# Weight loading and splitting of a mixture-of-experts kernel put at fixed places, and part of the routing lists moved into the attention stage

## The chip, the cores and the metric

The kernel runs on one core of a Trainium2 chip. The metric is the device time of one execution in microseconds (us). Engines are named as the profile names them: PE (matrix products), PEld (loading the weights into PE), DVE (vector), ACT (scalar), POOL (the engine that issues the indexed gathers and scatters) and SP (the engine that issues the plain transfers). Each engine works through its own instructions in the order in which they were written.

## The reference, cut to what matters

```python
# attention with a decaying state: 4 batches, 8 heads, 768 steps, head size 48
for t in range(S):
    cur = einsum('bhd,bhe->bhde', u * kt, vt)
    y[:, :, t] = einsum('bhd,bhde->bhe', rt, state + cur)
    state = w * state + einsum('bhd,bhe->bhde', kt, vt)
# mixture of experts on x = y as 3072 tokens of 384; 8 experts, hidden size 1024
noisy = x @ w_gate + log1p(exp(x @ w_noise)) * noise
top2 = the two largest of 8 per token; weights = softmax over the two
for e in range(8):
    h = maximum(x[mask] @ w1[e], 0)
    out[mask] += weight * (h @ w2[e])
```

All inputs and the output are float32. The kernel keeps that accuracy by writing each operand of a large product as a sum of two parts, high and low, and taking three products (high by high, high by low, low by high).

## The kernel before, in words

**Attention** (loop over 24 tiles of 128 tokens, `for i in range(NT)`). Per tile, PE makes transposes, scores (L353) and the output `py` (L395, L403); DVE masks the scores (`am`, L361) and adds up the tile's output `x` (L411), which goes to DRAM as `xd`. PE then makes router logits (L433). The routing of the tokens is done in three groups of 8 tiles by the generator `route(g)`, on DVE mainly: `rstep(us)` runs as many of its small steps as fit into a given time budget, so that they lie between the attention's own DVE operations.

**Lists.** Every expert needs the list of its tokens. `drop` makes a group's contribution: two compare operations for `oa` (L513), three for `ob` (L517, L520, L522), eight small PE products into `pL` (L526), and an addition to `L` (L532). For groups 1 and 2, `route` makes only the contribution to expert 0's list; the contribution to the lists of experts 1 to 7 is made by `rest(g)`, twice per group (first and second choice). Before the change `rest(1)` and `rest(2)` are both queued after the attention stage has ended and run inside the products of expert 0, by `rest_step`. When both are done, `rows` turns `L` into row numbers `GR` (L679), and `xgather(1, 0)` starts to gather expert 1's tokens.

**Experts.** Each expert's 832 places are taken in chunks: expert 0 in three (256, 256 and 320 columns), experts 1 to 7 in two (384 and 448 columns). A chunk has a first product `p1` (8 blocks f of the hidden size, 9 matmuls each into `ph`, L881, three PSUM buffers) and a second product `p2` (24 matmuls for each tile of 128 tokens into `pym`, L915, and 16 for the tile of 64, L906 and L908). After each block of `p1`, ACT takes the relu's high part (`hb`, and `ht` for the last 64 columns, L883) and DVE the low part (L885). After each tile of `p2`, ACT copies `pym` out to `ot` (L921), and `emit_out` scales it by the gate on DVE (L934 for expert 0; L932 for the others, which also adds what was in `out`) and scatters it with POOL (L936). For experts from 2 on, `spread` (L832) rearranges the next chunk's gathered tokens `xgt` into `xq` by 16 transfers on SP, DVE transposes them (L850), and ACT and DVE split them into `xh` and `xl` (L860, L861). `pgather` (L819) fetches the present `out` rows, and `xgather` (L810) the next tokens; both are on POOL.

**Weights.** The weights of an expert come in seven parts: three of `w1` (128x1024 each) and four of `w2` (two blocks of 384 columns each). Each part is loaded by SP into one of three staging buffers `stg` (L278, L281), split by ACT into the high part (L285) and by DVE into the low part (L287). Before the change `w_split` makes a generator per part, and `wstep`, called once after each block of `p1` and each tile of `p2`, moves up to three of them on by one step: load, two empty steps, high part, low part. So a part's high split stands on ACT a few blocks after its load was put on SP's queue, and the first three parts of expert e+1 are begun in expert e's first chunk, the other four in its second.

## Time and profile before

| | us |
|---|---|
| runs before | 660.16, 667.80, 665.02 (median 665.02) |
| profiled execution, its own time | 663.06 |
| its span, first to last instruction | 661.3 |
| PE busy | 620.0 (94% of the span) |
| DVE, ACT, POOL busy | 373.6, 265.1, 263.8 |
| mean granted PE clock | 0.978 of full speed |

The attention stage takes the first 175 us of the span, expert 0 the time up to 247.8 us, and experts 1 to 7 follow with 55 to 60 us each up to 650.4 us. Rows of the timeline give a start in us from the span's beginning, a duration in us, the engine, the line, the operation and what it writes and reads; in square brackets stands how long the engine was idle before it and what ended that idle time. Rows of stretches give the length, the busy time and instruction count of PE, PEld, DVE, ACT and POOL, the granted PE clock as a share of full speed, and the busy share and rate of the DMA engines.

### The profile page before, as it was taken

How to read it: one execution, taken by the hardware profiler on the slowest of the kernel's cores; microseconds unless marked ns; L12 is line 12 of the kernel's file. 1: busy time of each engine (PE TensorE's matmuls, PEld its weight loads, DVE VectorE, ACT ScalarE, POOL GpSimd, SP SyncE). 2: the span in 40 equal slices, each digit the busy share in tenths (PEclk: the TensorE clock that was granted, in tenths of full speed). 3: DMA queues.
4: the chain of work that ended last, by engine and by line, in shares of the span. 5: the costliest groups of instructions: out<-in, count | busy, mean ns of one | idle time of the engine just before them, and what ended most of it. 6: DMA issues, size and time to landing. Idle time of an engine off the chain costs nothing.

```text
span 661.3 us, 12051 instructions
## 1 busy us (share of the span) xinstructions
PE 620.0 (94%) x4310; PEld 588.1 (89%) x4311; DVE 373.6 (56%) x925; ACT 265.1 (40%) x737; POOL 263.8 (40%) x389
## 2 busy tenths in 40 slices
PE   7899899989998789999899999999999999999993
PEld 5789899988898789999799988998999899899993
DVE  8787878699379945253526454462645536254330
ACT  1465656675322524242334334243342424333310
POOL 8587445544201237323532452263254227315111
PEclk8999879999999999999899999999999999999997
DMA  7997657654305534445643745374364446533100
GB/s 125 216 229 169 151 132 166 166 134 129 92 1 151 164 103 119 115 146 130 160 141 111 180 112 166 106 182 149 106 181 120 155 125 162 170 90 105 37 10 29
DMA packets 135350, 86.56 MB, mean 131 GB/s; under 512 B 110625, under 2 KB 125345, under 8 KB 135282
## 3 DMA queue, kind: packets, MB, share of 16 engines
q1 hardware_dynamic: 125346, 56.87, 34.5%
q0 software_dynamic: 9936, 28.83, 14.5%
q8 instruction: 36, 0.59, 0.4%
q14 instruction: 32, 0.26, 0.1%
HBM read 59.03 MB, written 19.76 MB: 119 GB/s over the span
## 4 chain that ended last, share of the span: by engine, by line
PE 35%; SPq 14%; DMA 8%; DVE 7%; ACT 4%; issue 4%; POOL 2%; POOLq 0%; DVEq 0%; ACTq 0%
PE pym L915 17%; PE ph L881 15%; SPq L832 12%; DMA stg<-in_moe_w_dram 5%; SPq L281 2%; DMA pv<-out_dram,GA 2%; DVE xl L861 1%; DMA xgt<-xd,GR 1%; ACT xh L860 1%; POOL pv L819 1%; ACT w1h L285 1%; PE pym L908 1%; DVE ot L932 1%; PE pym L906 1%; DVE hb L885 1%
## 5 line engine op out<-in xcount | busy, mean ns | idle before, releaser
L915 PE MATMUL pym<-w1h,hb 128*128 128x384 f32 x768 | 202.3, 341 | 5.3 <-DVE hb L885 3.5
L885 DVE SCALAR_TENSOR_TENSOR hb<-ph,hb 128x384 fp32r<-128x384 f32 (+1 forms) x136 | 72.4, 533 | 143.4 <-ACT ht L883 83.3
L915 PEld LDWEIGHTS pym<-w1h,hb 128*128 128x128 f32 x768 | 139.8, 190 | 8.5 <-DVE hb L885 5.9
L881 PE MATMUL ph<-xh,w0h 128*128 128x384 f32 (+3 forms) x408 | 141.3, 346 | 5.8 <-DVE ht L885 4.0
L881 PE MATMUL ph<-xl,w0h 128*128 128x384 f32 (+3 forms) x408 | 140.0, 343 | 0.5 <-DVE xl L861 0.4
L881 PE MATMUL ph<-xh,w0l 128*128 128x384 f32 (+3 forms) x408 | 139.6, 342 | 0.0
L936 POOL DMA_INDIRECT out_dram<-ot,TK x56 | 57.5, 1027 | 192.6 <-DVE ot L932 154.7
L915 PE MATMUL pym<-w1l,hb 128*128 128x384 f32 x384 | 130.0, 339 | 0.0
L883 ACT ACTIVATE hb<-ph 128x384 fp32r<-128x384 f32 (+1 forms) x136 | 63.2, 469 | 96.3 <-PE ph L881 95.3
L881 PEld LDWEIGHTS ph<-xh,w0h 128*128 128x128 f32 x408 | 77.3, 189 | 11.0 <-issue 3.3
L881 PEld LDWEIGHTS ph<-xl,w0h 128*128 128x128 f32 x408 | 77.3, 190 | 3.6 <-DVE xl L861 1.2
L881 PEld LDWEIGHTS ph<-xh,w0l 128*128 128x128 f32 x408 | 77.5, 190 | 2.7
L915 PEld LDWEIGHTS pym<-w1l,hb 128*128 128x128 f32 x384 | 72.7, 189 | 0.1
L403 PE MATMUL py<-vt,am 128*128 128x96 f32 x384 | 60.3, 283 | 5.8 <-DVE am L361 4.8
L819 POOL DMA_INDIRECT pv<-out_dram,GA x49 | 53.2, 1085 | 31.0 <-issue 15.4
L810 POOL DMA_INDIRECT xgt<-xd,GR x42 | 43.6, 1038 | 40.9 <-DMA xq<-xgt 25.5
L921 ACT ACTIVATE ot<-pym 128x384 f32<-128x384 f32 x45 | 22.0, 489 | 92.7 <-PE pym L915 92.7
L403 PEld LDWEIGHTS py<-vt,am 128*128 128x128 f32 x384 | 51.7, 197 | 7.8 <-DVE am L361 7.8
L314 POOL TENSOR_TENSOR kd<-kt,tabk 128x192 f32<-128x192 f32 x46 | 27.8, 625 | 61.7 <-PE pwarm L371 50.4
L861 DVE TENSOR_TENSOR xl<-xq,xh 128x384 fp32r<-128x384 f32 (+1 forms) x42 | 22.3, 530 | 31.3 <-ACT xh L860 31.3
L860 ACT ACTIVATE xh<-xq 128x384 fp32r<-128x384 f32 (+1 forms) x42 | 21.0, 500 | 44.9 <-DVE xq L850 44.9
L810 POOL DMA_INDIRECT xg<-xd,GR x14 | 13.7, 982 | 59.6 <-DVE f L688 34.0
(217 smaller groups left out, 910.7 us busy)
## 6 DMA issues: line engine op xcount, KB each, us to landing
stg<-in_moe_w_dram SPq DMA_DIRECT2D x32, 384.0 KB, 4.4
stg<-in_moe_w_dram SPq DMA_DIRECT2D x72, 128.0 KB, 3.4
xq<-xgt SPq DMA_DIRECT2D x144, 36.0 KB, 1.9
rd<-in_r_dram SPq DMA_DIRECT2D x24, 192.0 KB, 4.0
vt<-in_v_dram SPq DMA_DIRECT2D x24, 192.0 KB, 4.0
xd<-x SPq DMA_DIRECT2D x24, 192.0 KB, 2.0
out_dram<-zrow SPq DMA_DIRECT2D x16, 288.0 KB, 3.8
kt<-in_k_dram SPq DMA_DIRECT2D x23, 192.0 KB, 3.6
```

Of the source, the lines that this page charges most:

```text
L314: (eng or nc.gpsimd).tensor_mul(kd[i % 3][:, h, :D], kt[i][:, h], tabk[:, h, :D])
L403: nc.tensor.matmul(o2, AM[i][:, s, p, :], vt[i][:, h, None, :].to_broadcast([128, 2, D]), start=not c and h == 0, stop=h == H - 1, skip_gr ...
L810: nc.gpsimd.indirect_dma_start(out=xg[:n], out_offset=None, in_=xd[:GROUPS[GEARLY - 1][1] * 128] if early_ else xd, in_offset=bass.Indirec ...
L819: nc.gpsimd.indirect_dma_start(out=pv[:n], out_offset=None, in_=out, in_offset=bass.IndirectOffsetOnAxis(ap=GA[:n, e * NJ + t:e * NJ + t + ...
L832: nc.sync.dma_start(xq[32 * a:32 * a + 32, q:w_:4], XGT[e, ci][32 * q:32 * q + 32, :m, a * 96:(a + 1) * 96])
L860: nc.scalar.activation(xh[:, g], v, AF.Copy)
L861: nc.vector.tensor_sub(xl[:, g], v, xh[:, g].bitcast(F32))
L881: nc.tensor.matmul(ph[:, :w_], a[:, d, fs], x[:, :w_ // 32, d], start=(j == 0), stop=(j == len(q) - 1))
L883: nc.scalar.activation(h_[:, f, 0, :], ph[:, a:b], AF.Relu)
L885: nc.vector.scalar_tensor_tensor(h_[:, f, 1, :], ph[:, a:b], 0.0, h_[:, f, 0, :].bitcast(F32), op0=ALU.max, op1=ALU.subtract)
L915: nc.tensor.matmul(py, hb[:, f, a, hs], x[:, f, :], start=(j == 0), stop=(j == len(q) - 1))
L936: st = nc.gpsimd.indirect_dma_start(out=out, out_offset=bass.IndirectOffsetOnAxis(ap=TK[:n, q:q + 1], axis=0), in_=ot[:n], in_offset=None, ...
```

## The change

It does five things:

1. **Weight parts at fixed places.** `wstep` is kept for expert 0 alone. For the others `w_p2`, called ahead of each second product, puts three loads on SP's queue (parts 0 to 2 of expert e+1 ahead of every second product but the last of expert e; parts 4 to 6 ahead of the last), and `w_p1`, called after each block j of a first product, does the splits: in an expert's first chunk parts 4 to 6 of the same expert at j = 0 to 5 (high part at even j, low part at odd j), in its last chunk parts 0 to 3 of the next expert at j = 0 to 7, with part 3 loaded at j = 2. No split stands in a second product any more.
2. **`rest(1)` begins in the attention stage.** It is queued at tile 22, and what is left of it is finished before `route(2)` is queued. `rest(2)` stays where it was.
3. **Expert 0's scaling** moves from DVE (L934) to ACT.
4. **`spread` is a generator.** Its 16 transfers are put out three at a time, one lot per block of the first product.
5. **Expert 1's first chunk** may be transposed inside expert 0's last second product if the lists are done by then (`next(xt)` twice per tile), and `tile_counts` (a small PE product and nine small DVE operations) moves from the end of expert 0's second chunk to the end of its third.

```diff
-                if mat or e < ESP:
-                    nc.sync.dma_start(tv, src)
-                else:
-                    for a in range(4):
-                        nc.sync.dma_start(tv[32 * a:32 * a + 32, 0, :], src[a])
+                nc.sync.dma_start(tv, src)
...
+    def w_load(e, k):
+        if e >= E:
+            return
+        t = stg.tile([128, 1024], F32, name="stg")
+        WS[e, k] = t
+        if k < ND:
+            if e >= ESP:
+                src = w1[e].rearrange("(a c j) f -> c a j f", a=4, j=32)[k]
+                for a in range(4):
+                    nc.sync.dma_start(t[32 * a:32 * a + 32, :], src[a])
+            else:
+                nc.sync.dma_start(t, w1[e, k * 128:(k + 1) * 128, :])
+        else:
+            c = 2 * (k - ND)
+            nc.sync.dma_start(t[:, :2 * DM].rearrange("p (c d) -> p c d", d=DM),
+                              w2[e, c * 128:(c + 2) * 128, :].rearrange("(c p) d -> p c d", p=128))
...
+    def w_hi(e, k):
+        if e < E:
+            tv, hi, _ = w_view(e, k)
+            nc.scalar.activation(hi, tv, AF.Copy)
+
+    def w_lo(e, k):
+        if e < E:
+            tv, hi, lo = w_view(e, k)
+            nc.vector.tensor_sub(lo, tv, hi.bitcast(F32))
+
+    def w_p1(e, ci, j):
+        if ci == 0:
+            if j < 6:
+                (w_lo if j % 2 else w_hi)(e, ND + 1 + j // 2)
+        elif ci == len(chunks(e)) - 1:
+            k = j // 2
+            (w_lo if j % 2 else w_hi)(e + 1, k)
+            if j == 2:
+                w_load(e + 1, ND)
+
+    def w_p2(e, ci):
+        last = ci == len(chunks(e)) - 1
+        for k in range(ND):
+            w_load(e + 1, ND + 1 + k if last else k)
...
                                   XGT[e, ci][32 * q:32 * q + 32, :m, a * 96:(a + 1) * 96])
+                if (4 * q + a) % 3 == 2:
+                    yield
...
-            nc.vector.tensor_scalar(ot[:n], ot[:n], g, None, op0=ALU.mult)
+            nc.scalar.activation(ot[:n], ot[:n], AF.Copy, scale=g)
...
             if b == i + 1:
+                while g == GEARLY and route_q:
+                    rstep(1)
...
             early()
+            route_q.append(rest(GEARLY - 1))
...
-    tile_counts(CAP)
     att_stack.close()
...
-    wq.extend(w_split(1))
-    for _ in range(3):
-        wstep()
+    w_p2(0, 0)
     att_pool[0] = late[0]
-    route_q.append(rest(GEARLY - 1))
     route_q.append(rest(GEARLY))
...
+        sd = spread(*seq[s + 1]) if sp[0] else iter(())
         for j, _ in enumerate(p1(e, ci)):
             while hold:
                 emit_out(*hold.pop(0))
-            if j == 0 and sp[0]:
-                spread(*seq[s + 1])
+            next(sd, None)
...
-            wstep()
+            w_p1(e, ci, j)
+        for _ in sd:
+            pass
         if s > 2 and s + 2 < len(seq):
             xgather(*seq[s + 2])
+        w_p2(e, ci)
...
+            if s == 2 and listed[0]:
+                for _ in range(2):
+                    next(xt, None)
...
-            wstep()
             hold.append((e, t))
...
             xgather(*seq[s + 2])
+            tile_counts(CAP)
```

How the order of the instructions changes is shown at three places. In these rows stand the line, the operation, what it writes and reads, its shape, and how often it stands in a row; lines are those of each kernel's own file, so that the same operation has another number after the change.

ACT, in the second first product of an expert (448 columns; the same in experts 2 to 6). `hb` and `ht` are the relu of one block, `GT` the gates, `w0h` and `w1h` the high parts of `w1` and `w2`. Before:

```order
L883 ACTIVATE hb<-ph 128x384
L883 ACTIVATE ht<-ph 128x64
L837 ACTIVATE GT<-xgt 128x1 x3
L883 ACTIVATE hb<-ph 128x384
L883 ACTIVATE ht<-ph 128x64
L285 ACTIVATE w1h_4977<-stg 128x768
L883 ACTIVATE hb<-ph 128x384
L883 ACTIVATE ht<-ph 128x64
L285 ACTIVATE w1h_4977<-stg 128x768
L883 ACTIVATE hb<-ph 128x384
L883 ACTIVATE ht<-ph 128x64
L285 ACTIVATE w1h_4977<-stg 128x768
```

And after the change, from the first block on:

```order
L936 ACTIVATE hb<-ph 128x384
L936 ACTIVATE ht<-ph 128x64
L336 ACTIVATE w0h_4958<-stg 128x1024
L936 ACTIVATE hb<-ph 128x384
L936 ACTIVATE ht<-ph 128x64
L936 ACTIVATE hb<-ph 128x384
L936 ACTIVATE ht<-ph 128x64
L890 ACTIVATE GT<-xgt 128x1 x3
L336 ACTIVATE w0h_4958<-stg 128x1024
L936 ACTIVATE hb<-ph 128x384
L936 ACTIVATE ht<-ph 128x64
L336 ACTIVATE w0h_4958<-stg 128x1024
```

The three splits of `w2` in a row, after blocks 3 to 5, are gone; splits of the next expert's `w1`, loaded a whole second product earlier in the program, stand after every second block.

SP, at the same place of the program: `xq<-xgt` are the 16 transfers of `spread`, `32x1024` a quarter of a `w1` part, `128x2x384` a `w2` part. Before:

```order
L281 DMA stg<-in_moe_w_dram 32x1024 x12
L832 DMA xq<-xgt 32x3x96 x16
L278 DMA stg<-in_moe_w_dram 128x2x384 x4
L832 DMA xq<-xgt 32x4x96 x8
L832 DMA xq<-xgt 32x3x96 x8
```

And after the change:

```order
L315 DMA stg<-in_moe_w_dram 32x1024 x12
L883 DMA xq<-xgt 32x3x96 x9
L320 DMA stg<-in_moe_w_dram 128x2x384
L883 DMA xq<-xgt 32x3x96 x7
L320 DMA stg<-in_moe_w_dram 128x2x384 x3
L883 DMA xq<-xgt 32x4x96 x8
L883 DMA xq<-xgt 32x3x96 x8
```

SP's order is nearly what it was; one load of `w2` has moved in among the 16 transfers.

DVE, from the last two attention tiles into expert 0's first product (`x` and `am` belong to the attention, `xl` is the low part of expert 0's first tokens, `c` and `GR` belong to tile 22 and before). Before:

```order
L679 TENSOR_SCALAR GR<-lt 128x4
L328 TENSOR_REDUCE c_2558<-rku 128x8
L411 TENSOR_TENSOR x<-py,cv 128x384
L361 TENSOR_TENSOR am<-pa,mneg 128x512 x2
L411 TENSOR_TENSOR x<-py,cv 128x384
L861 TENSOR_TENSOR xl<-ptm,xh 128x384 x2
L885 SCALAR_TENSOR_TENSOR hb<-ph,hb 128x256 x3
```

And after the change, from the fifth small operation of `rest(1)` on:

```order
L592 TENSOR_SCALAR r_ej<-SLI 128x16
L564 TENSOR_TENSOR r_oa<-r_mm,im 128x512 x2
L462 TENSOR_TENSOR x<-py,cv 128x384
L568 TENSOR_TENSOR r_ob<-r_ej,ij 128x8x49
L571 TENSOR_TENSOR r_ob<-r_ob,thi 128x8x49
L412 TENSOR_TENSOR am<-pa,mneg 128x512 x2
L573 TENSOR_SCALAR r_ob<-r_ob,pcol 128x8x49
L462 TENSOR_TENSOR x<-py,cv 128x384
L583 TENSOR_TENSOR L<-L,pL 128x2x49
L564 TENSOR_TENSOR r_oa<-r_mm,im 128x512 x2
L568 TENSOR_TENSOR r_ob<-r_ej,ij 128x8x49
L914 TENSOR_TENSOR xl<-ptm,xh 128x384 x2
```

The list's operations now stand between the attention's last operations and ahead of `xl`; three more of them (`r_ob` twice and `L`) follow around the first `hb`.

## Rows read from the trace of the kernel before

**Rows 1.** ACT's high splits of `w1`, whole span: busy us, mean ns | idle before.
```profile
L285 ACT ACTIVATE w0h<-stg 128x1024 fp32r<-128x1024 f32 x24 | 25.3, 1059 | 29.5 <-DMA stg<-in_moe_w_dram 29.5
```
**Rows 2.** ACT and PE in expert 3's second first product (the timeline).
```profile
403.44 0.85 ACT L285 ACTIVATE w1h<-stg 128x768 fp32r<-128x768 f32 x1 [3.54 <-DMA stg<-in_moe_w_dram]
...
405.65 0.45 PE L881 MATMUL ph<-xh,w0h 128*128 128x448 f32 x1 [0.89 <-DVE ht L885]
```
**Rows 3.** SP's timeline there: spreads, then loads.
```profile
389.65 10.23 SPq L832 DMA_DIRECT2D xq<-xgt  x16
399.92 6.88 SPq L278 DMA_DIRECT2D stg<-in_moe_w_dram  x4
```
**Rows 4.** Stretches (length, five engines' busy time, clock, DMA): experts 2-6, products.
```profile
305.12:594.94 289.82, 280.42 (x1521) 268.79 (x1521) 138.45 (x265) 107.85 (x260) 114.07 (x140) 0.99 0.51 142
...
391.76:407.55 15.79, 14.90 (x73) 13.45 (x73) 5.31 (x13) 6.36 (x19) 5.22 (x6) 1.00 0.57 172
407.55:423.06 15.51, 15.51 (x89) 15.19 (x88) 8.21 (x17) 4.89 (x12) 2.29 (x4) 1.00 0.30 86
594.94:607.58 12.64, 12.64 (x74) 12.64 (x73) 5.51 (x10) 4.29 (x12) 6.91 (x8) 1.00 0.35 94
607.58:620.06 12.48, 12.48 (x74) 12.48 (x73) 5.41 (x11) 3.19 (x7) 4.10 (x7) 1.00 0.23 76
620.06:634.76 14.70, 14.70 (x73) 13.53 (x73) 5.35 (x15) 4.72 (x15) 1.06 (x2) 1.00 0.04 15
```
**Rows 5.** The stretch of expert 0 from its second chunk's second product on.
```profile
203.99:247.76 43.77, 36.91 (x240) 34.44 (x236) 32.78 (x101) 15.03 (x40) 12.83 (x19) 0.96 0.48 145
```
**Rows 6.** PE's timeline in that stretch: where it stood still.
```profile
211.33 0.52 PE L526 MATMUL pL<-xgt 128*128 128x98 bf16 x8 [1.54 <-DVE xgt L522]
...
228.22 0.53 PE L526 MATMUL pL<-xgt 128*128 128x98 bf16 x8 [2.56 <-DVE xgt L522]
...
246.64 0.55 PE L858 MATMUL ptm<-ident,xg 128*128 128x128 f32 x3 [1.30 <-DVE xl L861]
247.76 0.44 PE L881 MATMUL ph<-xh,w0h 128*128 128x384 f32 x1 [0.58 <-ACT xh L860]
```
**Rows 7.** Two stretches in which PE's clock was lowered (columns as in rows 4).
```profile
78.00:90.00 12.00, 11.30 (x74) 10.65 (x75) 7.87 (x32) 4.48 (x17) 2.81 (x6) 0.57 0.57 129
228.00:234.00 6.00, 5.78 (x33) 5.79 (x34) 4.32 (x12) 1.73 (x5) 0.00 (x0) 0.72 0.73 200
```
**Rows 8.** DVE's timeline: one half of a `rest`, up to its PE products.
```profile
207.46 0.27 DVE L487 TENSOR_TENSOR r_os<-OH,SLF 128x128 f32<-128x128 f32 x1
...
208.54 1.29 DVE L513 TENSOR_TENSOR xgt<-r_mm,im 128x512 bf16<-128x512 int32 x2
209.75 0.56 DVE L517 TENSOR_TENSOR xgt<-r_ej,ij 128x392 bf16<-128x392 int32 x1
...
210.95 0.33 DVE L522 TENSOR_SCALAR xgt<-xgt,pcol 128x392 bf16<-128x392 bf16 x1
```
**Rows 9.** DVE's timeline at the end of attention.
```profile
167.71 0.56 DVE L411 TENSOR_TENSOR x<-py,cv 128x384 f32<-128x384 f32 x1 [1.54 <-issue]
169.41 1.29 DVE L361 TENSOR_TENSOR am<-pa,mneg 128x512 int32<-128x512 int32 x2 [1.14 <-PE pa L353]
...
174.78 1.03 DVE L861 TENSOR_TENSOR xl<-ptm,xh 128x384 fp32r<-128x384 f32 x2 [0.91 <-ACT xh L860]
177.52 0.42 DVE L885 SCALAR_TENSOR_TENSOR hb<-ph,hb 128x256 fp32r<-128x256 f32 x1 [1.71 <-ACT hb L883]
```
**Rows 10.** PE's timeline there: transposes of expert 0's tokens, and its second matmul.
```profile
173.73 0.82 PE L858 MATMUL ptm<-ident,xg 128*128 128x128 f32 x6
...
175.86 0.38 PE L881 MATMUL ph<-xl,w0h 128*128 128x256 f32 x1 [0.21 <-DVE xl L861]
```
**Rows 11.** ACT's copies out of the second product (page, costliest groups).
```profile
L921 ACT ACTIVATE ot<-pym 128x384 f32<-128x384 f32 x45 | 22.0, 489 | 92.7 <-PE pym L915 92.7
```
**Rows 12.** Loads of `w2` parts (page, DMA issues): count, size, us to landing.
```profile
stg<-in_moe_w_dram SPq DMA_DIRECT2D x32, 384.0 KB, 4.4
```

More of the change, by code (lines that the diff above doesn't have):

```diff
@@ L291, in w_split @@
         for c in range(ND):
[L292 to L293 removed]
+            units.append(unit(0, c, c + 1, w1[e, c * 128:(c + 1) * 128, :].rearrange("(c p) f -> p c f", p=128)))
         for c in range(0, NF, 2):
@@ L307, in wstep, with w_view @@
             wrun.append(un)
+    WS = {}
+    def w_load(e, k):
[14 more added lines that the diff above has]
+                              w2[e, c * 128:(c + 2) * 128, :].rearrange("(c p) d -> p c d", p=128))
+    def w_view(e, k):
+        mat = int(k >= ND)
+        if mat not in W.setdefault(e, {}):
+            sh = [128, NF, DM] if mat else [128, ND, FF]
+            W[e][mat] = [wpool[e % 2].tile(sh, F32R, name=f"w{mat}{x}{e % 2}", bufs=1) for x in "hl"]
+        c = slice(2 * (k - ND), 2 * (k - ND) + 2) if mat else slice(k, k + 1)
+        hi, lo = (t[:, c, :] for t in W[e][mat])
+        tv = WS[e, k][:, :hi.shape[1] * hi.shape[2]].rearrange("p (a b) -> p a b", b=hi.shape[2])
+        return tv, hi, lo
+    def w_hi(e, k):
[19 more added lines that the diff above has]
+            w_load(e + 1, ND + 1 + k if last else k)
     AM, X, CV, PY, PA = {}, {}, {}, {}, {}
@@ L1102 @@
         end = s + 1 == len(seq)
-        if e and ci == 0:
-            nxt = w_split(e + 1) if e + 1 < E else []
-            wq.extend(nxt[:ND])
-        elif e:
-            wq.extend(nxt[ND:])
         xt = xT(*seq[s + 1]) if not end else iter(())
         sp = [x < len(seq) and seq[x][0] >= ESP for x in (s + 1, s + 2)]
+        sd = spread(*seq[s + 1]) if sp[0] else iter(())
         for j, _ in enumerate(p1(e, ci)):
```

4 lines of the change are left out of this document (removed).

## The prediction

> **What bounds the kernel now.** I read the busy times first: PE is busy for 620.0 of 661.3 us, so only what makes PE stand still or run slowly can be won. Then the waits of each engine. PE's own waits are short ones for DVE and ACT, but ACT, whose high splits of `w1` take 1.06 us each, stands idle for 29.5 us in all before these 24, waiting for loads [rows 1]. The timeline shows how this reaches PE. ACT stood 3.54 us before the split of a `w2` part because its load had not landed; the relu of the next block was queued behind it, DVE's low part behind the relu, and PE, out of PSUM buffers, stood 0.89 us [rows 2]. The load was late because SP had put it out only after the 16 transfers of `spread`, which took it 10.23 us, from 389.65 to 399.92 [rows 3]; the block at which the split stood came only a few microseconds later.
>
> Next the stretches product by product, to see what that costs [rows 4]. Expert 7 has no successor, so nothing is split in it: its first three products take 12.64, 12.48 and 14.70 us. Expert 3's second first product, the same matmuls, takes 15.79. Expert 3's last product takes 15.51 and PE never stands in it. The five experts 2 to 6 take 289.82 us together.
>
> Last, expert 0's stretch from 203.99 to 247.76 us: 43.77 us, in which DVE is busy for 32.78 [rows 5]. Here PE waits for DVE's list operations and for the first tokens of expert 1: 1.54, 2.56, 1.30 and 0.58 us [rows 6]. After the wait of 2.56 the granted clock averages 0.72 over 228 to 234 us, the lower of its two levels (1.2 instead of 2.4 GHz) for part of it [rows 7]: 6 us by 0.28 is 1.7 us of matmul time lost.
>
> **The change part by part.**
>
> *Splits at fixed places, experts 2 to 6.* The same loads and splits are made; what goes is ACT's wait. Parts 0 to 2 are now split a whole second product after they are put on SP's queue, and parts 4 to 6 likewise, so each has over 12 us instead of a few. In the new first products every second block carries a high split on ACT and every other one a low split on DVE; in expert 3 the engines have room (ACT 6.36, DVE 5.31 of 15.79 us, with splits in it) [rows 4]. The second products lose their splits, and DVE and ACT there have only the next chunk's tokens to do. So I take expert 7's first three products and expert 3's last: 12.64 + 12.48 + 14.70 + 15.51 = 55.33 us per expert, five times 276.65, against 289.82: **-13.2 us**. The bounds: at best the first product also runs at the 12.48 of its twin, -14.0; at worst the splits, which still share ACT and DVE with the relu, keep half of the stalls alive, -6.6.
>
> *Part 3 of each expert* is the one that keeps a short lead: it is loaded at block 2 and split at block 6 of the same first product, and on SP it stands behind nine transfers of `spread` and behind the buffer that block 1's low split frees. In expert 3 the product began at 391.76 [rows 4]; with the stall of the one before it gone, it would begin some 1.5 us earlier, at 390.3. Nine of 16 issues from 389.65 take 5.8 us, to 395.4 [rows 3]; block 1's low split ends at about 396.5 (two blocks of 14.70 / 8 = 1.84 us, then relu, low part and the split itself, some 2.5 together). Landing takes 4.4 us [rows 12]: 400.9. Block 6 is done on PE after 7 x 1.84, and on ACT at about 403.8. That leaves 2.9 us; I cost it at nothing.
>
> *Expert 0's stretch.* `rest(1)` leaves it, and so do `tile_counts` and the scaling on DVE. Of the four waits all should go: the first was for the first list batch, which now begins sooner on DVE because `tile_counts` and its nine operations no longer stand ahead of it; the second was for the second group's batch; the last two were for expert 1's tokens, which could only be transposed after the last matmul and now have the whole last product for it. -1.54 - 2.56 - 1.30 - 0.58 [rows 6], the clock -1.7 [rows 7], and two batches of list matmuls that leave, 0.35 each, -0.7: **-8.4 us**. Bounds: -5 if one of the larger waits comes back; -10 if the rest of the stretch (a wait of some 0.8 us for `xh` at the third chunk's start and shorter ones) tightens as well.
>
> *The attention's end* has to carry what left. On DVE a half of `rest` takes 1.08 us of small operations, 1.21 for `oa`, 1.2 for two of `ob` and 0.33 for the last [rows 8]. Ahead of the last tile's `am` DVE was idle for 1.54 + 1.14 = 2.68 us [rows 9]; 1.08 + 1.21 + 1.2 = 3.5 us now stand there, so `am`, and PE's product behind it, come 0.8 us late. The first batch's matmuls, 0.35, go ahead of the transposes, which started at 173.73 [rows 10]: now 174.9. They end one batch's matmuls earlier, so `L` (0.25), `oa` (1.21) and one `ob` (0.6) run from 175.0 and `xl` starts at 177.1 instead of 174.78 [rows 9], 2.3 us late; PE's second matmul, at 175.86 [rows 10], waits for it just so long. Behind block 0 come the router's products (0.6) and then the second batch, which needs the low part of block 0 and one more operation on DVE (0.42 + 0.33, after a relu): in the old order DVE begins that low part at 177.52, 0.5 after the block [rows 9], so PE stands another 0.7, and the batch itself takes 0.35. Together **+3.4 us**. Bounds: +0.7 if only the matmuls count; at worst two waits as long as the longest list wait, 2 x 2.56 [rows 6], with the 0.7 and the clock lowered as at 78 to 90 us, where 12 us at 0.57 lost 5.2 [rows 7]: +11.
>
> *At nothing.* `tile_counts` ahead of expert 1's first product: one small product and nine operations on at most eight numbers, each under the 0.27 of rows 8, so at most 2.4 us on DVE; three PSUM buffers of 12.48 / 8 = 1.56 us of matmuls each cover it, and without them it would cost its surplus, some 0.8 us once. The scaling on ACT: four copies of 128x384, 0.49 each by the copies of the same size [rows 11], 2.0 us after block 0 of expert 0's third chunk, with a split of 1.06 behind; with a block every 1.3 us (12.64 / 8 by 320 / 384 columns) PE needs block 1's buffer again only three blocks later, so there is just room. The Trainium skill (ScalarE: Activation LUTs, Rules for kernel authors) speaks against this edit: it gives multiplications to the vector engine, and prices an ACTIVATE at about 0.3 us and 0.83 ns per element, by an estimate 0.62 us here. No row shows this form on ACT; the copies' 0.49 lie below it. By the page the four would take 0.5 us more than the room, and the sum would be 0.5 us higher; it does not enter it.
>
> **The sum.** 663.06 (the profiled execution's own time) - 13.2 - 8.4 + 3.4 = **644.9 us**. The median of the runs shown is 2.0 us higher (665.02) and they spread over 7.6, so a median of new runs may sit a little beside it. At least 1% (some 6.6 us) is needed for a measurement of this kernel to tell a change from none.
>
> **The rivals.**
>
> *Buffers, not loads.* PE's stalls in the experts could come from having three PSUM buffers for `ph` and stay wherever the splits stand. For it: the stall ends with a buffer coming free [rows 2]. Against it: expert 7, with the same three buffers, has none [rows 4]. Then only expert 0's terms count: 663.06 - 8.4 + 3.4 = 658.1 us. The Trainium skill has this as a rule (Perfetto Trace Analysis, Optimization Strategy): the same gap repeating on the engine that should be full can mean too few buffers for the next tile. By that rule the stalls stay; the trace agrees only that the gap repeats. Chance 0.06.
>
> *Half of the stalls stay.* A split of 1.06 us on ACT between two relus, with gates and tokens beside it, may still make a block late. 644.9 + 6.6 = 651.5 us. For it: ACT's relu and DVE's low part lie in one chain [rows 2]; against it the room in rows 4. Chance 0.10.
>
> *The end of attention costs the worst.* 644.9 + 11 - 3.4 = 652.5 us. For it: both waits of rows 6 that are longest are list waits, and one lowered the clock. Chance 0.13.
>
> *Slower: part 3 is late in every expert.* The nine transfers ahead of it wait for the gathered tokens, which come at the end of POOL's row of scatters and gathers. If this row ends later than the 2.9 us of slack, and some 2.6 more that PE has in its buffers (ACT's 3.54 cost PE 0.89, [rows 2]), ACT stands at block 6 and PE with it. With PE standing as long as ACT did there, 3.54, and the clock falling as at 228 us, 1.7, six experts (1 to 6 prepare a successor) lose 31.4: 676.3 us. It decides from 5.5 us of lateness on. Against it: SP began the transfers at 389.65, before the product began [rows 3, 4], and nothing on POOL is added. Chance 0.03.
>
> **How the numbers follow.** My forecast has the remaining 0.68. All but the first rival (0.7% faster, within 1%) and the last are faster by over 1%: 0.68 + 0.10 + 0.13 = 0.91; within 1%: 0.06; slower: 0.03. Single terms at their better bounds give 663.06 - 14.0 - 10 + 0.7 = 639.8, and the runs' spread reaches 1 or 2 us past it; upwards the two rivals at 651.5 and 652.5 are taken in, those at 658.1 and 676.3 (0.09 together) are not. Range 638 to 654 us.
>
> **What would show it.** Right: ACT's waits for `stg` nearly gone; experts 2 to 6 at 55 to 56 us each; no wait of PE over 1 us in expert 0 after its second product; the lists' matmuls in two batches near 175 us, with PE idle for about 2 us there in place of 0.6; expert 1's first product beginning about 5 us earlier than 247.76 us. Wrong: PE stalls of 0.8 us or more that repeat in every expert, on `hb` or `ht`; an ACT wait of several us before a `w1h` split at block 6; the clock lowered around 175 to 185 us.

## The result and the profile after

The changed kernel takes 641.16 us (median of 4 runs, 638.52 to 643.36), the kernel before 662.59 beside it (median of 4, 658.99 to 667.80): a ratio of 0.967 with a 95% interval of 0.958 to 0.976. The forecast was 644.9 us, faster. The profiled execution took 643.36 us, its span is 641.6. A ratio, here and below, compares only runs within 1.5% of the fastest of their kernel.

The page of the changed kernel: the engines' busy time, PE's granted clock in 40 slices, and the chain of work that ended last, by engine:

```profile
PE 615.3 (96%) x4310; PEld 588.7 (92%) x4311; DVE 375.1 (58%) x918; ACT 269.5 (42%) x744; POOL 261.3 (41%) x389
...
PEclk9979969999989999999999999999999999999998
...
PE 69%; DVE 2%; ACT 1%; issue 0%; POOL 0%; POOLq 0%; ACTq 0%
```

PE's idle time fell from 41.3 to 26.3 us (the span less the busy time), 15.0 of the 19.7 us by which the span is shorter. Transfers and SP's queue have left the chain; before, it was:

```profile
PE 35%; SPq 14%; DMA 8%; DVE 7%; ACT 4%; issue 4%; POOL 2%; POOLq 0%; DVEq 0%; ACTq 0%
```

ACT's high splits of `w1`, grouped by line; L281 is expert 0's loading, L336 all the others:

```profile
L336 ACT ACTIVATE w0h<-stg 128x1024 fp32r<-128x1024 f32 x21 | 22.3, 1063 | 0.0
...
L281 ACT ACTIVATE w0h<-stg 128x1024 fp32r<-128x1024 f32 x3 | 3.2, 1058 | 7.3 <-DMA stg<-in_moe_w_dram 7.2
```

Where ACT stood 29.5 us ahead of these splits [rows 1], it stands 7.3, all of it in expert 0's own weights. The next rows are stretches, as in [rows 4, 5]: experts 2 to 6 together; then three of expert 3's four products (the second product of its first chunk, the first and the second of its last); then expert 0's stretch:

```profile
300.51:575.83 275.32, 275.32 (x1521) 268.13 (x1521) 140.66 (x265) 109.03 (x260) 111.69 (x140) 1.00 0.54 150
368.03:380.51 12.48, 12.48 (x73) 12.48 (x73) 5.40 (x11) 3.19 (x7) 8.07 (x11) 1.00 0.69 193
380.51:395.22 14.71, 14.71 (x74) 13.52 (x73) 8.74 (x18) 8.59 (x22) 0.99 (x1) 1.00 0.38 106
395.22:410.73 15.51, 15.51 (x89) 15.19 (x88) 5.86 (x11) 3.55 (x8) 6.08 (x9) 1.00 0.54 154
208.29:243.50 35.21, 34.05 (x226) 32.21 (x222) 21.18 (x65) 14.40 (x41) 12.21 (x17) 1.00 0.40 129
```

In experts 2 to 6 PE is busy for the whole 275.32 us. The second first product takes 14.71 us with the splits in it, as expert 7's does without any. In expert 0's stretch PE's timeline has only two waits, and neither is one of [rows 6]:

```profile
219.14 0.41 PE L934 MATMUL ph<-xh,w0h 128*128 128x320 f32 x1 [0.76 <-ACT xh L913]
225.74 0.39 PE L934 MATMUL ph<-xh,w0h 128*128 128x320 f32 x1 [0.22 <-DVE ht L938]
```

The end of attention pays for it. PE's timeline and then DVE's (columns as in [rows 9, 10]), and two stretches with the granted clock:

```profile
171.06 1.06 PE L454 MATMUL py<-vt,am 128*128 128x96 f32 x4 [0.83 <-DVE am L412]
...
178.10 0.39 PE L934 MATMUL ph<-xl,w0h 128*128 128x256 f32 x1 [1.18 <-DVE xl L914]
```

```profile
175.18 0.26 DVE L583 TENSOR_TENSOR L<-L,pL 128x98 f32<-128x98 f32 x1 [0.40 <-PE pL L577]
175.35 1.28 DVE L564 TENSOR_TENSOR r_oa<-r_mm,im 128x512 bf16<-128x512 int32 x2
176.56 0.56 DVE L568 TENSOR_TENSOR r_ob<-r_ej,ij 128x392 bf16<-128x392 int32 x1
177.03 1.01 DVE L914 TENSOR_TENSOR xl<-ptm,xh 128x384 fp32r<-128x384 f32 x2
```

```profile
178.00:182.00 4.00, 3.90 (x24) 3.72 (x25) 1.36 (x5) 0.57 (x2) 0.00 (x0) 0.58 0.01 4
180.00:184.00 4.00, 4.00 (x32) 3.77 (x31) 1.34 (x4) 0.77 (x3) 0.00 (x0) 0.75 0.01 2
```

`xl` stands behind the second half's `L`, `oa` and one `ob`, and behind the wait of 1.18 us that this makes, the clock averages 0.58 of full speed over 4 us.

### The profile page after: what moved, and what is told of

It reads as the page before. It is cut to its first block, busy times and chain, and to the rows that moved or that the text cites. A ratio compares the mean times of both kernels' runs of the same rounds, so it can differ in the third digit from the quotient of the medians.

```text
span 641.6 us, 12126 instructions
## 1 busy us (share of the span) xinstructions
PE 615.3 (96%) x4310; PEld 588.7 (92%) x4311; DVE 375.1 (58%) x918; ACT 269.5 (42%) x744; POOL 261.3 (41%) x389
## 4 chain that ended last, share of the span: by engine, by line
PE 69%; DVE 2%; ACT 1%; issue 0%; POOL 0%; POOLq 0%; ACTq 0%
PE ph L934 33%; PE pym L968 31%; PE pym L961 2%; PE pym L959 2%; PE ptm L911 0%; DVE r_oa L564 0%; DVE xl L914 0%; ACT ot L987 0%; PE pL L577 0%; PE pl L484 0%; PE py L454 0%; DVE hb L938 0%; ACT w0h L336 0%; DVE r2q L511 0%; ACT hb L936 0%
## 5 line engine op out<-in xcount | busy, mean ns | idle before, releaser
L968 PE MATMUL pym<-w1h,hb 128*128 128x384 f32 x768 | 199.9, 337 | 0.0
L934 PE MATMUL ph<-xh,w0h 128*128 128x384 f32 (+3 forms) x408 | 140.3, 344 | 1.4 <-ACT xh L913 1.2
L934 PE MATMUL ph<-xl,w0h 128*128 128x384 f32 (+3 forms) x408 | 139.3, 341 | 1.3 <-DVE xl L914 1.2
L934 PE MATMUL ph<-xh,w0l 128*128 128x384 f32 (+3 forms) x408 | 139.3, 341 | 0.0
L934 PEld LDWEIGHTS ph<-xh,w0h 128*128 128x128 f32 x408 | 76.9, 189 | 5.0 <-ACT xh L913 1.5
L934 PEld LDWEIGHTS ph<-xl,w0h 128*128 128x128 f32 x408 | 76.9, 189 | 4.3 <-DVE xl L914 1.7
L934 PEld LDWEIGHTS ph<-xh,w0l 128*128 128x128 f32 x408 | 76.9, 189 | 2.8
L861 POOL DMA_INDIRECT xgt<-xd,GR x42 | 41.8, 996 | 65.3 <-DMA xq<-xgt 24.6
L412 DVE TENSOR_TENSOR am<-pa,mneg 128x512 int32<-128x512 int32 x48 | 30.7, 680 | 10.0 <-PE pa L404 10.0
L861 POOL DMA_INDIRECT xg<-xd,GR x14 | 15.1, 1079 | 50.5 <-DVE f L739 37.4
```

The costliest lines, as they stand in the source:

```text
L412: nc.vector.tensor_tensor(am[:, s].bitcast(I32), pa[s].bitcast(I32), mneg.to_broadcast([128, NP, 128]), op=ALU.bitwise_and)
L861: nc.gpsimd.indirect_dma_start(out=xg[:n], out_offset=None, in_=xd[:GROUPS[GEARLY - 1][1] * 128] if early_ else xd, in_offset=bass.Indirec ...
L934: nc.tensor.matmul(ph[:, :w_], a[:, d, fs], x[:, :w_ // 32, d], start=(j == 0), stop=(j == len(q) - 1))
L968: nc.tensor.matmul(py, hb[:, f, a, hs], x[:, f, :], start=(j == 0), stop=(j == len(q) - 1))
```

## How the runs are compared

The runs of the kernel before spread from 653.5 to 676.5 us over the study, and so times of different kernels can't settle 1 or 2 us. The traces show one source of it: in the kernel before and the changed one the clock averages 0.83 over 60 to 90 us (0.17 of 30 us is 5.1), in other executions 1.00 with the same wait of 1.85 us for `am` in it. The two rows are that stretch in the changed kernel and in the run called "xl first" below:

```profile
60.00:90.00 30.00, 28.02 (x275) 26.39 (x274) 21.87 (x64) 15.74 (x56) 12.42 (x23) 0.83 0.56 131
```

```profile
60.00:90.00 30.00, 28.01 (x333) 26.33 (x333) 24.73 (x89) 19.16 (x69) 13.66 (x25) 1.00 0.64 153
```

The last attention tile's first score matmul starts at 168.2 us before the change, at 168.4 in the changed kernel and at 163.2 in "xl first"; over all executions it starts between 161.8 and 168.9, and hardly anything that the change touches lies before it. So the profiled executions are compared from that matmul on, and the time from it to the end of the span is called the remainder. The table gives the stretches from the first matmul of each to that of the next, in us: to expert 0's first product; its first three products; the stretch of [rows 5]; expert 1; experts 2 to 6; expert 7 with the end of the span; and their sum, the remainder. The names are those of the next section, where "not finished" is the run that leaves the first group's rest unfinished. Each row is one execution; where two kernels have the same code, as the first, third and fourth row in the first stretches, they agree within 0.1 us.

| kernel | tile starts | to product | three products | expert 0 | expert 1 | 2 to 6 | 7, end | remainder |
|---|---|---|---|---|---|---|---|---|
| before | 168.21 | 7.06 | 28.72 | 43.77 | 57.36 | 289.82 | 66.38 | 493.1 |
| changed | 168.39 | 8.15 | 31.75 | 35.21 | 57.01 | 275.32 | 65.78 | 473.2 |
| weights alone | 164.03 | 7.06 | 28.75 | 44.20 | 57.45 | 275.32 | 66.23 | 479.0 |
| loads first | 162.19 | 7.05 | 28.75 | 43.77 | 57.46 | 275.32 | 66.00 | 478.4 |
| lists alone | 168.89 | 7.91 | 31.70 | 36.40 | 62.06 | 290.18 | 65.84 | 494.1 |
| not finished | 167.34 | 8.15 | 30.69 | 35.23 | 57.01 | 275.32 | 66.11 | 472.5 |
| no step in last tile | 162.37 | 7.78 | 31.26 | 35.48 | 57.90 | 276.01 | 65.86 | 474.3 |
| part 3 at block 5 | 162.36 | 8.15 | 31.72 | 35.48 | 58.65 | 275.41 | 65.60 | 475.0 |
| spread at once | 168.73 | 8.15 | 30.76 | 35.53 | 58.58 | 275.77 | 65.84 | 474.6 |
| scaling on DVE | 161.81 | 8.15 | 31.65 | 35.88 | 58.68 | 276.07 | 65.89 | 476.3 |
| rest(1) after attention | 166.44 | 7.40 | 28.70 | 47.21 | 58.89 | 275.76 | 65.83 | 483.8 |
| rest(1) cut in two | 162.18 | 8.15 | 28.71 | 39.88 | 61.03 | 275.73 | 66.18 | 479.7 |
| counts back | 163.88 | 8.15 | 30.74 | 36.77 | 56.92 | 275.27 | 65.83 | 473.7 |
| xl first | 163.20 | 7.78 | 29.20 | 35.20 | 57.01 | 275.32 | 65.97 | 470.5 |

## The experiments

**Weights alone.** The kernel before with part 1 and the lots of `spread` (parts 2, 3 and 5 left out).

```diff
+    w_p2(0, 0)
-    wq.extend(w_split(1))
...
-            wstep()
+            w_p1(e, ci, j)
...
+        w_p2(e, ci)
```

> Before, with part 1 of the change (fixed places of loads and splits) and the lots of spread, but lists, scaling and counts as before. My theory (the wins of experts 2 to 6 and of expert 0 are separate): experts 2 to 6 take about 275 us, 14 less than before; the list waits of expert 0's stretch stay (1.5 to 2.6 us each), the end of attention keeps its 10.5 us long first product; time about 14 us below before, ratio 0.978 to 0.98. Rival (the stalls come from three PSUM buffers and not from the place of the splits): experts 2 to 6 stay at 285 to 290 us, ratio above 0.99.

647.05 us, ratio 0.979 (0.971 to 0.986). Experts 2 to 6 take 275.32 us, expert 0's stretch 44.20 with its two list waits still there (1.54 and 2.21), the end of attention what it did before. The experts' gain of 14.5 us comes with part 1 (the lots of `spread`, part 4, are in this run too, and "spread at once" below finds them worth next to nothing), and the stalls do not come from the number of PSUM buffers, which is three here as before.

**Loads first.** The kernel before; only the loads move, no split does.

```diff
+    def wstart():
+        n = len(wrun)
+        while wq and len(wrun) < 3:
+            un = wq.pop(0)
+            next(un)
+            wrun.append(un)
+            wait[un] = len(wrun) - n
...
             if j == 0 and sp[0]:
+                wstart()
                 spread(*seq[s + 1])
```

> Before, with one edit: up to three loads of weight parts are put on SP's queue ahead of the 16 transfers of spread; every split stays where it stood in the program, on ACT and DVE. My theory (late loads make the stalls, wherever the splits stand): most of ACT's 82 us of waiting for stg ahead of splits goes, experts 2 to 6 take 276 to 280 us, time 10 to 14 us below before. Rival (the bunched places of the splits, three high parts after blocks 3 to 5, make the stalls): experts 2 to 6 stay at 287 to 290 us. Second rival (the loads wait for staging buffers that the splits free, so that they hold the transfers behind them up): the gathered tokens come late and the time rises by some us.

643.60 us, ratio 0.973 (0.967 to 0.979): most of the whole change. Experts 2 to 6 take the same 275.32 us. On ACT, DVE, PE and POOL the trace has every instruction in the same order as before the change; SP's order alone differs. ACT's three splits of `w2` stand one behind each of three blocks, and none waits; the rows are the first two:

```profile
387.26 0.85 ACT L285 ACTIVATE w1h<-stg 128x768 fp32r<-128x768 f32 x1
388.61 0.49 ACT L895 ACTIVATE hb<-ph 128x384 fp32r<-128x384 f32 x1 [0.50 <-PE ph L893]
389.00 0.22 ACT L895 ACTIVATE ht<-ph 128x64 fp32r<-128x64 f32 x1
389.10 0.85 ACT L285 ACTIVATE w1h<-stg 128x768 fp32r<-128x768 f32 x1
```

SP has put three loads out some 12 us ahead of the transfers; behind those it has none until the splits free a buffer. ACT's waits ahead of splits, by group over the whole span, are gone but for expert 0's own:

```profile
364.48 3.56 SPq L278 DMA_DIRECT2D stg<-in_moe_w_dram  x3
376.84 10.24 SPq L844 DMA_DIRECT2D xq<-xgt  x16
390.87 0.37 SPq L278 DMA_DIRECT2D stg<-in_moe_w_dram  x1
```

```profile
L285 ACT ACTIVATE w1h<-stg 128x768 fp32r<-128x768 f32 x32 | 27.1, 846 | 0.2
L285 ACT ACTIVATE w0h<-stg 128x1024 fp32r<-128x1024 f32 x24 | 25.2, 1055 | 6.1 <-DMA stg<-in_moe_w_dram 6.1
```

So the short lead between load and split is the whole cause of the stalls in experts 2 to 6: with longer leads the splits cost nothing in their old places, and by "weights alone" nothing in the new ones. The second rival is out too: the gathered tokens do not come late, and the time does not rise.

**Lists alone.** The changed kernel with the weights, and `spread`, as before.

```diff
-            w_p1(e, ci, j)
+            wstep()
...
-        w_p2(e, ci)
```

> The changed kernel with the weights loaded and split as before, and spread in one lot; lists, scaling and counts as after the change. My theory: experts 2 to 6 back at about 290 us with ACT's waits for stg, expert 0's stretch some 8 us shorter than before, the end of attention some 4 us longer; time 4 to 5 us below before, ratio about 0.993. Rival (expert 0's stretch became shorter only because the splits left it too): the stretch wins less than 4 us and the time is within 1 us of before.

660.79 us, ratio 0.997 (0.994 to 1.001): no change, so my 4 to 5 us did not come, nor is the rival right, since the stretch wins more than 4. The stretch does shrink, by 7.4 us, and the end of attention costs 3.8 as in the changed kernel; but expert 1 takes 4.7 us more. SP's row and ACT's and PE's there:

```profile
271.19 11.25 SPq L888 DMA_DIRECT2D xq<-xgt  x16
282.55 6.63 SPq L278 DMA_DIRECT2D stg<-in_moe_w_dram  x4
```

```profile
285.81 0.84 ACT L285 ACTIVATE w1h<-stg 128x768 fp32r<-128x768 f32 x1 [5.97 <-DMA stg<-in_moe_w_dram]
```

```profile
288.01 0.71 PE L939 MATMUL ph<-xh,w0h 128*128 128x448 f32 x1 [3.31 <-DVE ht L943]
```

With expert 0 shorter, PE reaches expert 1's second first product 3.2 us earlier (271.69; before the change 274.93), but the tokens that POOL gathers for `spread` are there no earlier: the transfers begin at 271.19, where they began at 270.79. So they begin 0.5 us ahead of the product and not 4.1, the loads stand behind them, and ACT waits 5.97 us. The load went out 0.11 us behind the last transfer (271.19 + 11.25 = 282.44). The Trainium skill (DMA: Bandwidth & Descriptors, Anatomy of one DMA, which is on transfers issued by POOL) says that any semaphore wait happens on the issuing sequencer before dispatch; SP's row fits that, since what held the transfers back held the loads behind them. So the two large parts are not independent: in this run the list part pays nothing without early loads.

**First group's rest not finished ahead of the second group's routing.**

```diff
-                while g == GEARLY and route_q:
-                    rstep(1)
```

> The changed kernel without finishing the first group's rest ahead of the second group's routing at the last attention tile; its last steps then run in expert 0. My theory (the finishing put list operations ahead of the attention's last ones, cost 2 us of waiting and 1.7 us of lowered clock): the first product of expert 0 takes about 11 us again instead of 13.5 and begins up to 1 us earlier; 1 to 4 us faster than the changed kernel, 639 to 642 against 643. Rival: the lists end later for it, PE waits 1 to 2.5 us for them in expert 0's second and third chunk, and the time is within 1 us of the changed kernel or above it.

639.76 us, ratio 0.966 (0.960 to 0.972); the remainder is 0.7 us shorter. The first product takes 12.49 us, not 11: PE still waits 1.18 us for `xl`, so the finishing was not what held it, and that the time fell into my range was luck. The microsecond against 13.54 is the clock: "spread at once" and "counts back" keep the finishing, and their first products take 12.55 and 12.51 us with the clock at 1.00.

**No list step in the last tile.** As the run before, and the last attention tile's two lots of list steps are left to expert 0.

```diff
-        rstep(STEPS_A)
+        if i < NT - 1:
+            rstep(STEPS_A)
...
-        rstep(STEPS_B)
+        if i < NT - 1:
+            rstep(STEPS_B)
```

> The changed kernel without finishing the first group's rest ahead of the second group's routing, and with no list step at all in the last attention tile, so that am and xl have DVE to themselves there. My theory (each list operation ahead of am or xl on DVE makes PE late by its own time): the wait of 0.83 for am and the one of 1.18 for xl go, expert 0's first product begins 0.8 us earlier and takes 10.5 to 11.5 us instead of 12.5; 2 us faster than the run without the finishing, 638 in the same conditions. Rival (the lists are now one half later and end too late): waits of 1 to 2.5 us for list operations come back in expert 0's second and third chunk and the gain is below 0.5 us.

638.67 us, ratio 0.964 (0.959 to 0.970); remainder 474.3, 1.8 more than the run before. Only 0.45 of the 1.8 lie between the last tile and the end of expert 0; the rest came in the experts behind it, which the edit does not touch. The gain of 2 us did not come. Both theories were half right: the wait for `xl` went back to its old size (0.20), but the one for `am` stayed, because the operations ahead of it stand in the tile before; and PE's wait ahead of expert 0's own list matmuls grew from 0.70 to 1.76 us, since the second group's routing is behind them on DVE.

**xl first.** Only the last tile's second lot of list steps is left to expert 0, so the first half stays ahead of `xl` and the second comes behind it.

```diff
-                while g == GEARLY and route_q:
-                    rstep(1)
...
-        rstep(STEPS_B)
+        if i < NT - 1:
+            rstep(STEPS_B)
```

> The changed kernel without finishing the first group's rest ahead of the second group's routing, and without the second of the last attention tile's lots of list steps, so that xl stands ahead of the second half's L, oa and ob on DVE. Counted from the last tile's first score matmul (changed 473.2, without the finishing 472.5). My theory: the wait of 1.18 for xl becomes the 0.2 that it was before the change, expert 0's first product takes 10.9 to 11.5 us, the routing behind it ends up to 0.5 us later; remainder 471.3 to 472.0, the best of all. Rival (the routing is what sets the end of expert 0's second first product, and every list operation behind xl delays it): the wait ahead of that product's list matmuls grows from 0.7 to 1.7 us or more and the remainder is 472.5 or more.

635.26 us (6 runs), ratio 0.962 (0.957 to 0.966); remainder 470.5, the shortest of all and 0.8 below my range. PE's waits at the end of attention, then the stretches up to expert 0's first product and of that product:

```profile
165.87 1.06 PE L454 MATMUL py<-vt,am 128*128 128x96 f32 x4 [0.83 <-DVE am L412]
171.57 0.39 PE L934 MATMUL ph<-xl,w0h 128*128 128x256 f32 x1 [0.21 <-DVE xl L914]
```

```profile
163.20:170.98 7.78, 6.79 (x67) 6.08 (x66) 4.58 (x10) 1.87 (x7) 2.87 (x3) 1.00 0.60 180
170.98:181.98 11.00, 10.79 (x94) 10.47 (x94) 7.94 (x26) 4.39 (x14) 0.00 (x0) 1.00 0.01 3
```

It wins 2.7 us on the changed kernel from the last tile on, of which about 1.0 is the clock that did not fall; the list matmuls behind the routing wait 0.70 us, as in the changed kernel, so the rival is out. The intervals of the two ratios overlap, so by times alone they aren't told apart; both are faster than before.

**First group's rest after attention.** The changed kernel without part 2.

```diff
             early()
-            route_q.append(rest(GEARLY - 1))
...
+    route_q.append(rest(GEARLY - 1))
     route_q.append(rest(GEARLY))
```

> The changed kernel without part 2: the first group's rest is queued after the attention stage again, ahead of the second group's; all else as changed. Times are counted from the first score matmul of the last attention tile to the end of the span, which leaves the attention's own spread out (before 493.1, changed 473.2). My theory (part 2 only moves DVE work, since the lists have some 8 us of slack in expert 0 once the splits and the counts are out of their way): the end of attention costs what it did before (7.1 us to the first product, which takes 10.5), expert 0's stretch takes 36 to 38 us, and the remainder is 470 to 472. Rival (part 2 is what makes the list waits go): two waits of 1.5 to 2.6 us on list operations come back, the stretch takes 39.5 us or more and the remainder is 473.5 or more.

649.03 us, ratio 0.983 (0.975 to 0.991), remainder 483.8. My theory fell, and of the rival's two list waits one came back (2.21), the other long wait is for tokens: without part 2 the remainder is 10.6 us longer (1.9 of it in expert 1, for a cause that stays open), and the stretch is longer than before the change (47.21). PE's waits in it:

```profile
222.23 0.39 PE L934 MATMUL ph<-xh,w0h 128*128 128x320 f32 x1 [0.65 <-DVE w0l L341]
225.99 0.54 PE L577 MATMUL pL<-xgt 128*128 128x98 bf16 x8 [2.21 <-DVE xgt L573]
238.68 0.90 PE L911 MATMUL ptm<-ident,xg 128*128 128x128 f32 x3 [3.30 <-DMA xg<-xd,GR]
```

Two halves more are some 7 us of DVE by [rows 8] (1.08, and twice 1.21, 1.2, 0.33 and the addition of 0.25), but the second group's last addition to `L` ends 31.7 us into the stretch and not 14.1 as in the changed kernel: the list batches reach into the third chunk, as before the change, where the low splits of expert 1's weights (1.22 us each) and the relus stand between their operations. The tokens are there only at 238.68, and the transposes, which part 5 put inside the last second product, hold PE for 3.30 us. Behind that wait the clock falls:

```profile
238.00:244.00 6.00, 4.93 (x17) 4.53 (x18) 1.12 (x2) 1.16 (x4) 1.04 (x2) 0.50 0.24 70
```

It averages 0.89 over the stretch. "Weights alone", which differs from this run by parts 3 and 5, has nearly the same idle time of PE there (7.2 us of 44.20, here 7.7 of 47.21) but a clock of 0.96. So what makes this stretch the longer one is, by an estimate from these clocks (5.2 against 1.8 us lost), the clock and not a longer wait.

**First group's rest cut in two.** The first half where the change put it, the second after attention.

```diff
-            route_q.append(rest(GEARLY - 1))
+            route_q.append(rest(GEARLY - 1, (0,)))
...
+    route_q.append(rest(GEARLY - 1, (1,)))
     route_q.append(rest(GEARLY))
```

> The changed kernel with the first group's rest cut in two: its first half where the change put it, its second half (with the two small operations that begin it made again) after the attention stage, ahead of the second group's. Counted as for the run before. My theory: the wait for am (0.83) stays, the wait of 1.18 for xl and the second batch's wait in expert 0's first product go (10.5 to 11 us), expert 0's stretch takes 35 to 37 us, remainder 471 to 472.5. Rival (every list operation left for expert 0 comes back as a wait): the stretch grows by the 3.3 us that the half takes on DVE, remainder 474 or more.

643.84 us, ratio 0.974 (0.963 to 0.986), remainder 479.7. The first product takes 10.50 us, as before the change, but the stretch grows by 4.7, with a wait of 2.38 us at a list batch: the rival, though 4.0 of the remainder's 6.5 us stand in expert 1 and have an open cause. The same half, some 3.3 us of DVE, cost 2.0 in expert 0's first product (10.50 against the 12.5 of executions without the clock's fall) and 4.7 in the stretch, of which 1.6 is the clock by an estimate (0.74 over 221 to 227 us, behind the wait).

**Counts back.** `tile_counts` at the end of expert 0's second chunk again.

```diff
+    tile_counts(CAP)
     att_stack.close()
...
             xgather(*seq[s + 2])
-            tile_counts(CAP)
```

> The changed kernel with the counts (a small PE product and nine small DVE operations) at the end of expert 0's second chunk again. My theory (the first list batch waited 1.5 us before the change because the counts stood ahead of it): a wait of 1 to 2 us ahead of the first list batch comes back, the stretch of expert 0 takes 36.2 to 37.5 us instead of 35.2 to 35.5. Rival (the wait came from the first group's rest alone): no wait over 0.3 us there, 35.2 to 35.6 us.

639.30 us (one run), the stretch 36.77. PE's row at the first list batch:

```profile
210.11 0.52 PE L577 MATMUL pL<-xgt 128*128 128x98 bf16 x8 [1.53 <-DVE xgt L573]
```

The wait of 1.54 us [rows 6] is back to a hundredth, and with it the 1.56 us of the stretch: the counts and their nine small operations made it.

**Scaling on DVE.**

```diff
-            nc.scalar.activation(ot[:n], ot[:n], AF.Copy, scale=g)
+            nc.vector.tensor_scalar(ot[:n], ot[:n], g, None, op0=ALU.mult)
```

> The changed kernel with expert 0's scaling on DVE again instead of ACT. My theory (part 3 of the change is hidden): expert 0's stretch from its second chunk's second product to expert 1's first product takes 35.2 us plus or minus 0.5. Rival (the scaling on DVE holds the list operations back and so the tokens of expert 1): PE waits over 1 us for lists or tokens again and the stretch takes 37 us or more.

640.01 us (one run). The stretch takes 35.88 us, 0.2 past my bound and far from the rival's 37. PE does not wait for lists or tokens; it waits 0.89 us (0.22 in the changed kernel) at a block of the third chunk for DVE's `ht`, with the scaling and the row numbers ahead of it on DVE:

```profile
219.73 0.38 PE L934 MATMUL ph<-xh,w0h 128*128 128x320 f32 x1 [0.89 <-DVE ht L938]
```

Part 3 wins some 0.4 to 0.7 us against the 35.20 to 35.53 us of the runs that have the lists as changed.

**Spread at once.** All 16 transfers at block 0.

```diff
-            next(sd, None)
+            if j == 0:
+                for _ in sd:
+                    pass
```

> The changed kernel with the 16 transfers of spread put out in one lot at the first block, as before; part 3's load then stands behind all 16 instead of 9 on SP, some 4.5 us later. My theory (part 4 of the change only makes room for part 3's load): ACT waits about 1 us for it in every expert, PE does not, experts 2 to 6 at 275 to 276 us. Rival (the lots matter for the next chunk's tokens too): PE waits for xh or xl at the start of first products, 280 us or more.

645.18 us (one run). Part 3's load goes out 7.95 us into expert 3's product (changed 6.39), ACT waits for it once in the whole span, 1.2 us in expert 1, and not in every expert, and experts 2 to 6 take 275.77, against 275.32: in this one execution part 4 is worth nothing to speak of.

**Part 3 at block 5.**

```diff
-            if j == 2:
+            if j == 5:
```

> The changed kernel with part 3 of each next expert loaded at block 5 of the last first product instead of block 2: on SP it is issued behind 15 or 16 transfers, about 5 us later, some 2 us too late for its split at block 6. My theory (PE has 2.6 us of cover in its buffers): ACT waits 1.5 to 2.5 us ahead of one w1h split in each of experts 1 to 6 (9 to 15 us in all), PE's waits in experts 2 to 6 stay under 0.3 us and the five take 275 to 277 us. Rival (any wait of ACT reaches PE in full): 1.5 to 2.5 us per expert, experts 2 to 6 at 283 to 288 us.

639.23 us (one run). SP's row in expert 3, whose product starts at 376.32, and ACT's splits of `w2` over the span:

```profile
375.26 10.23 SPq L883 DMA_DIRECT2D xq<-xgt  x16
385.60 8.29 SPq L320 DMA_DIRECT2D stg<-in_moe_w_dram  x4
```

```profile
L336 ACT ACTIVATE w1h<-stg 128x768 fp32r<-128x768 f32 x28 | 23.5, 839 | 0.3 <-DMA stg<-in_moe_w_dram 0.3
```

The load is 2.9 us later than in the changed kernel (9.28 into the product, not 6.39), not 5. SP does not keep PE's pace: it puts the 16 transfers out in one row, from 1.06 us ahead of the product on, and the load right behind them. And in the changed kernel the load did not follow its nine transfers at once, it went out 3.47 us behind them, when block 1's low split (DVE 385.63 to 386.84) had freed the buffer:

```profile
377.71 5.72 SPq L883 DMA_DIRECT2D xq<-xgt  x9
386.90 0.39 SPq L320 DMA_DIRECT2D stg<-in_moe_w_dram  x1
```

ACT waits 0.3 us in all. So part 3 has nearly 2.9 us of slack, but PE's cover behind it was not reached, and the 5.5 us from which the slower rival decides remain untried.

## Why the prediction was right

By the remainder the change wins 493.1 - 473.2 = 19.9 us; the forecast was 18.2 (13.2 + 8.4 - 3.4). Term by term:

- *Experts 2 to 6, -13.2:* measured -14.50, somewhat past the best bound. The four products fell to 12.5 to 12.6, 12.5, 14.6 to 14.7 and 15.3 to 15.5 us, as put together from experts 7 and 3. The mechanism is shown by "loads first": the late load, and nothing about the splits' places or buffers. "Half of the stalls stay" and "buffers, not loads" are both out. The forecast followed the wait in the second first product only, and the five of those won 5.2 us; 9.3 came from the second product of the first chunk, which took 13.0 to 17.4 us before. The cause there is the same, loads of `w1` that come late, and the sum holds it because it was made of whole products. Expert 2 before the change, the product and then ACT and PE in it:

```profile
317.60:335.00 17.40, 14.80 (x74) 13.87 (x73) 8.69 (x15) 5.94 (x11) 8.29 (x11) 0.90 0.47 131
321.20 1.06 ACT L285 ACTIVATE w0h<-stg 128x1024 fp32r<-128x1024 f32 x1 [2.03 <-DMA stg<-in_moe_w_dram]
322.68 0.44 PE L915 MATMUL pym<-w1h,hb 128*128 128x384 f32 x1 [1.80 <-ACT hb L883]
```

- *Expert 0's stretch, -8.4:* -8.56. All four waits went, and what took the first two away is shown: the moved counts and part 2. The last two went with tokens that come early and transposes that stand early (part 5); the run without part 2 shows PE waiting for tokens again. No run has early lists without part 5, so what each gave is not shown. The 0.8 for `xh` stayed, as the forecast had it. What it did not have is that the transposes of part 5 become a single long wait where the lists are late (3.30 us without part 2), with a fall of the clock behind it.
- *Attention's end, +3.4:* +4.1 (1.09 to the product, 3.05 in it, 0.02 less behind it). `am` waits 0.83 (forecast 0.8) and the second matmul starts 2.1 us later, counted from the last tile (forecast 2.3). The 0.7 ahead of the second batch did not come in this execution, in which the clock fell and PE itself reached the batch later. The forecast had that fall only in its worst case and named it as a sign of being wrong. Where the clock stayed at 1.00 ("spread at once", "counts back") the wait is there with 0.53 us, the product takes 12.5, and the term would have been 3.1. The row is from "counts back":

```profile
175.98 0.52 PE L577 MATMUL pL<-r_ob,r_oa 128*128 128x98 bf16 x8 [0.53 <-DVE r_ob L573]
```

- *At nothing:* part 3's load went out 6.39 us into the product (forecast 6.2, by 396.5 against 390.3), and the run that has it 2.9 us later, in which ACT waits 0.3, bears out the 2.9 us of slack. The counts and the scaling cost nothing where they are; where they were, they cost 1.5 and some 0.4 to 0.7. Four scalings in a row took 2.13 us on ACT (forecast 2.0); the seven in the trace are recorded with 613 ns each on average. The Trainium skill (ScalarE: Activation LUTs, Rules for kernel authors) makes one 0.62 us by an estimate, and the trace agrees for each by itself; in a row they overlap and follow each other every 0.51 us.

Expert 1 and the end, both outside the forecast, gave another 0.9 us. That the sum came within 1.7 us of the forecast is in part luck: 1.3 and 0.9 us more than forecast were won, 0.2 more in expert 0's stretch, and 0.7 more were lost at the end of attention, where the clock, which in other executions did not fall, cost 1.0.

## What to carry to other kernels

Where an engine waits for a load, look first at what stands ahead of that load on the queue that issues it: the loads of up to three weight parts moved ahead of 16 transfers gave 14.5 us in experts 2 to 6 with no compute instruction moved. Parts of a change that each look sound can depend on one another: the list part won nothing without early loads, and the early transposes held PE up where the lists were late. And where the runs spread more than the edit is worth, compare from a point that the edit does not touch.

## What was not expected

- The clock is not set by the order of the instructions alone. Six executions have the same list operations and PE waits of 0.83 or 0.58 and 1.18 us at the end of attention with the finishing kept; in four (changed, lists alone, scaling on DVE, part 3 at block 5) the clock fell behind the 1.18 (first product 13.5 us), in two (spread at once, counts back) it stayed at 1.00 (12.5). The same holds for the wait of 1.85 us at 77 to 79 us: behind it 78 to 90 us has a clock of 0.57 in the kernel before and in the changed one, and 1.00 in "loads first" and "xl first". The Trainium skill (TensorE: Matmul & The Clock Gate, What's actually happening) says, of the start of a kernel, that the window by which the gate judges runs free of it, so that one kernel measures differently from run to run. The rows agree that executions differ, here in the middle of a kernel; what decides it in one execution was not tried.
- In six of the runs (no step in last tile, part 3 at block 5, spread at once, scaling on DVE, and both runs with the rest moved) expert 1 takes 0.9 to 4.0 us longer than the changed kernel's 57.0. In "part 3 at block 5" ACT stood 7.02 us (in the changed kernel 3.58) before a copy out of the second product for a cause that the trace does not name, and PE waited 1.21 behind it; in the runs with the rest moved it stood 6.51 and 9.52, and PE waited 1.44 and 1.84. Whether this belongs to those kernels or to those executions stays open.
